# Decode attention with a gated MLP on one core: the first keys through two DMA queues, in halves of the partitions

## The chip, the core and the metric

The kernel runs on one core of a Trainium2 chip. The metric is the device time of one execution in microseconds. The kernel before takes 193.44 us (median of three runs, 193.33 to 193.98). All profile figures come from one profiled execution, and times inside it count from its first instruction. TensorE is PE (with PEld for its weight loads), VectorE is DVE, ScalarE is ACT, GpSimd is POOL and SyncE is SP. The suffix q (SPq, ACTq) means the sequencer that issues DMAs. SP and ACT each have a DMA queue of their own: q1 in the profile is SP's, q10 is ACT's.

## What is computed

One token (a row of 512) goes through a layer norm and then two branches: attention of 32 heads over the last 4096 positions of a key and value cache, and a small MLP. In the reference, cut to what matters:

```python
xn = _layernorm(x)
q = (xn @ wq).reshape(B, Sq, 32, 128)
W = 4096
k, v = k_cache[:, :, Sk - W:, :], v_cache[:, :, Sk - W:, :]
p = softmax(einsum("bhqd,bhkd->bhqk", q, k) * Dh ** -0.5)
s = einsum("bhqk,bhkd->bhqd", p, v).reshape(1, 1, 4096) @ wo
x1 = xn + shift(gelu(layernorm(xn) @ w1)) @ w2      # S = 1: the shifted rows are zero
g = silu(x1 + gelu(layernorm(x1) @ w3) @ w4)
out = x + s * g
```

Each of the 32 heads has 1 MiB of keys and 1 MiB of values, each read once. With the weights it is 79 MB in all, and little arithmetic on each byte.

## The kernel before, in words

The heads are worked in eight groups of four (G = 4, NG = 8). The keys of a group, K0 to K7 below, are one tile of 4 MiB, `kv` from `k_pool`: partition p = 4b + a holds positions 128b to 128b + 127 of head a, which is a row of 32 KB. The values V0 to V7 have the same form in `v_pool`. There are three key buffers (K_BUFS) and two value buffers (V_BUFS).

In the scores of a group, DVE takes the first 64 or 80 of the 128 positions of every partition: four times a product with the broadcast query (L321) and a sum over the 128 elements (L323), the function `k_vector`. PE takes the rest: it transposes pairs of positions (L339, `k_turn`), ACT copies them out (L342), and PE multiplies them with the query (L350, `k_scores`). Then follow the maximum (`sm_max`, L364 and L366), the exponential on ACT (`sm_exp`), the product with the values on PE (`v_wide`, L427) and the normalisation. A loop of NG + LAG = 10 steps writes the order out by hand for PE, DVE and ACT: in step s it works on the keys of group s and the values of group s - 2. In the last step the values of group 7 come in pieces (`cuts`, columns 0 to 64, 64 to 96 and 96 to 128), so that work starts on the first; the output weights of the last four heads come as rows (`load_rows`), and `y_head` multiplies with them.

Ahead of the loop stand the layer norms, the query (L208, from `wq`) and the MLP (L252 to L280). Their order on the engines is a scheduler's and not written out. The weights lie in a pool (`wts`) that is closed before V0 is loaded, since the value buffers take its place: so V0's load waits for all readers of the weights.

The loads have this order. ACT issues `x_bf`, `x_row` and `wq` (L79 to L84) and nothing more. SP issues w2, w3, w4 (1280 rows of it as 10 KB a partition, then 96 rows of 1 KB in one load of 96 partitions, L92), then K0 in two halves by columns (L534: positions 0 to 63 of each partition, then 64 to 127), K1, K2, V0, K3, V1, K4, V2 and so on. `keep_in_program_order` holds each queue to the order of the program. A load of keys from K3 on waits until the buffer of three groups before is read; a load of values waits for the buffer of two groups before. Loads share eight completion semaphores in turn, so a load can also wait until the eighth one before it has landed.

Of the kernel before, what the change touches and what calls it, by code (L numbers as in the profile page):

```python
# [8 lines left out]
P = 128  # L9
BF16 = mybir.dt.bfloat16  # L10
FP32 = mybir.dt.float32
ACT = mybir.ActivationFunctionType
ALU = mybir.AluOpType
# [5 lines left out]
G = 4  # L19
# [7 lines left out]
def kernel(  # L27
# [14 lines left out]
    nc = tc.nc  # L42
# [3 lines left out]
    _, H, Sk, Dh = A_k_cache.shape  # L46
# [3 lines left out]
    W0 = Sk - W  # L50
    assert W == 4096
    CP = G * W // P
    PB = P // G
# [3 lines left out]
    scale = float(Dh) ** -0.5  # L57


    k_pool = ctx.enter_context(tc.tile_pool(name="k", bufs=K_BUFS))  # L60
    kt_pool = ctx.enter_context(tc.tile_pool(name="kt", bufs=4))
    prod_pool = ctx.enter_context(tc.tile_pool(name="prod", bufs=1))
    const = ctx.enter_context(tc.tile_pool(name="const", bufs=1))
    small = ctx.enter_context(tc.tile_pool(name="small", bufs=1))
# [7 lines left out]
    wts_guard = tc.tile_pool(name="wts", bufs=1)  # L72
    wts = wts_guard.__enter__()

    def load(dst, src):
        return tc.keep_in_program_order(nc.sync.dma_start(out=dst, in_=src))  # L76

    x_bf = small.tile([P, KC], BF16, name="x_bf")
    nc.scalar.dma_start(out=x_bf[:], in_=A_x.rearrange("a b (p c) -> p (a b c)", p=P))  # L79
# [3 lines left out]
    wq_sb = wts.tile([P, KC, HD], BF16, name="wq_sb")  # L83
    nc.scalar.dma_start(out=wq_sb[:].rearrange("p c n -> p (c n)"),  # L84
                        in_=A_wq.rearrange("(a b c) n -> b a (c n)", a=4, c=KC))
    w2_sb = wts.tile([P, KC, D], BF16, name="w2_sb")
    load(w2_sb[:], B_w2.rearrange("(p c) n -> p c n", p=P))
    w3_sb = wts.tile([P, KC, F], BF16, name="w3_sb")
# [1 line left out]
    w4_sb = wts.tile([P, 11, D], BF16, name="w4_sb")  # L90
    load(w4_sb[:, 0:10, :], B_w4[0:10 * P, :].rearrange("(p c) n -> p c n", p=P))
    load(w4_sb[0:96, 10, :], B_w4[10 * P:F, :])  # L92


    def load_kv(pool, cache, g, cuts=(0, CP)):
        t = pool.tile([P, CP, Dh], BF16, tag="kv", name="kv")
        src = cache[0, G * g:G * g + G, W0:, :].rearrange("a (b c) d -> b a (c d)", b=PB)
        dst = t[:].rearrange("p c d -> p (c d)")
        for c0, c1 in zip(cuts, cuts[1:]):
            load(dst[:, c0 * Dh:c1 * Dh], src[:, :, c0 * Dh:c1 * Dh])  # L100
        return t
# [16 lines left out]
    nc.vector.tensor_copy(out=sel[:], in_=ident_bf[:, 0:P:32].unsqueeze(1).to_broadcast([P, PB, G]))  # L118
    ind = const.tile([P, 1], FP32, name="ind")
    nc.vector.tensor_reduce(out=ind[:], in_=ident_f[:, 0:P:32], axis=AX.X, op=ALU.max)  # L120
    neg_half = const.tile([P, 33], FP32, name="neg_half")
    nc.vector.memset(neg_half[:], -0.5)


# [27 lines left out]
    def rows_add(ps, col, w, last):  # L152
        k = col.shape[0]
        for j in range(KC):
            nc.tensor.matmul(ps[32 * j:32 * j + 1, :], lhsT=col, rhs=w[0:k, j * P:(j + 1) * P],
                             start=False, stop=last, skip_group_check=True)
# [60 lines left out]
    for b in range(2):  # L217
# [5 lines left out]
        for t in range(2):  # L223
            rows = slice(64 * t, 64 * t + 64)
            nc.scalar.copy(out=q_pair[rows, 4 * b:4 * b + 4, :, G * t:G * t + G].rearrange("p g l a -> p g a l"),
                           in_=qt_ps[rows].bitcast(BF16).rearrange("p g (a m l) -> p g a m l", a=G, l=2)[:, :, :, 0, :])
# [14 lines left out]
    xn_row = small.tile([P, P], FP32, name="xn_row")  # L241
# [26 lines left out]
    for i, (col, w) in enumerate(terms):  # L268
        r = 32 * (i % 4)
# [4 lines left out]
    h2_ps = ps_misc.tile([P, P], FP32, tag="misc", name="h2_ps")  # L274
    rows_open(h2_ps)
    rows_add(h2_ps, ind, hr, True)
    bv = small.tile([P, P], FP32, name="bv")
    nc.vector.tensor_tensor(out=bv[:], in0=xn_row[:], in1=h2_ps[:], op=ALU.add)
    g_row = small.tile([P, P], FP32, name="g_row")
    nc.scalar.activation(out=g_row[:], in_=bv[:], func=ACT.Silu)  # L280


    make_masks(16)
# [13 lines left out]
                            op=ALU.max)  # L297
    par_t = const.tile([1 + G, PB, G], FP32, name="par_t")
    nc.vector.tensor_scalar(out=par_t[:],
                            in0=ident_f[0:1 + G, 1:1 + G].unsqueeze(1).to_broadcast([1 + G, PB, G]),  # L300
# [26 lines left out]
    def batches(g):  # L327
        n, m = nd(g), CP - nd(g)
        k = -(-m // 8)
        edges = [n + 2 * (m // 2 * i // k) for i in range(k + 1)]  # L330
        return list(zip(edges, edges[1:]))
# [12 lines left out]
    def k_scores(g, b):  # L344
        kt = kts.pop(b)
        c0, c1 = batches(g)[b]
        for i in range((c1 - c0) // 2):
            c = c0 + 2 * i - nd(g)
            for l in range(2):
                nc.tensor.matmul(st[g]["sT"][:, c:c + 2, :].rearrange("p c a -> p (c a)"),  # L350
                                 lhsT=kt[:, i, l::2], rhs=q_pair[:, g, l, :], start=(l == 0), stop=(l == 1))
# [55 lines left out]
    def load_wo(i):  # L407
        h0, n = blocks[i]
        load(wo_blk[i], A_wo[h0 * P:(h0 + n) * P, :].rearrange("(p t) n -> p t n", p=P))
# [4 lines left out]
    def load_rows(h, n):  # L414
        load(wo_rows[:, h - h_part:h - h_part + n, :],
             A_wo[h * P:(h + n) * P, :].rearrange("(h p) n -> p h n", p=P))
# [108 lines left out]
    NG = H // G  # L525
# [5 lines left out]
    for s in range(NG + LAG):  # L531
        h = s - LAG
        last = h == NG - 1
        kn = load_kv(k_pool, A_k_cache, s, (0, 64, CP) if s == 0 else (0, CP)) if s < NG else None  # L534
        if s == LAG:
            wts_guard.__exit__(None, None, None)
            v_pool = ctx.enter_context(tc.tile_pool(name="v", bufs=V_BUFS))
            wo_blk[2] = v_pool.tile([P, 4, D], BF16, tag="wo_4", bufs=1, name="wo_4")
            wo_rows = v_pool.tile([P, H - h_part, D], BF16, tag="wo_rows", bufs=1, name="wo_rows")
        if last:  # L540
            v = load_kv(v_pool, A_v_cache, h, cuts)
            for r in (H - G, H - 2):
                load_rows(r, 2)
        elif h >= 0:
            v = load_kv(v_pool, A_v_cache, h)
        if h == 3:
            wo_24 = k_pool.tile([P, 32, D], BF16, tag="kv", name="wo_24")
            wo_blk[0], wo_blk[1] = wo_24[:, 0:16, :], wo_24[:, 16:24, :]
            load_wo(0)
        if h == 5:  # L550
            load_wo(1)
            load_wo(2)

        if s < NG:
            nb = len(batches(s))

            def keys(b0, b1):
                for b in range(b0, b1):
                    k_turn(s, kn, b)
                    if b > 0:  # L560
                        k_scores(s, b - 1)

            k_open(s)
            k_vector(s, kn, 0)
            keys(0, 2)
            if s == 7:
                v_turn(h - 1)
                v_add(h - 1)
                v_out(h - 1)
            elif s > 1:  # L570
                sm_den(s - 2)
                sm_rden(s - 2)
            elif s == 1:
                sm_max(0)
            k_vector(s, kn, 1)
            keys(2, 4)
            if s == 7:
                sm_den(h)
                sm_rden(h)
                keys(4, nb - 2)  # L580
                sm_turn(s - 1)
                keys(nb - 2, nb)
            else:
                if s > 0:
                    sm_turn(s - 1)
                keys(4, nb)
            k_scores(s, nb - 1)
            sm_own(s)
            if s == 7:
                k_vector(s, kn, 2)  # L590
                v_wide(h, v)
                sm_exp(s - 1)
                v_turn(h)
                y_open()
                k_vector(s, kn, 3)
                v_add(h)
                v_out(h)
                ox_spread(1)
                sm_max(s)
                continue  # L600
            if s > 0:
                sm_exp(s - 1)
            if h > 0:
                v_turn(h - 1)
            k_vector(s, kn, 2)
            if h >= 0:
                v_wide(h, v)
            if h > 0:
                v_add(h - 1)
                v_out(h - 1)  # L610
            if s == 6:
                ox_spread(0)
            k_vector(s, kn, 3)
            if s == 6:
                ox_pick(0)
            if s > 0:
                sm_max(s)
        elif s == NG:
            ox_pick(1)
            sm_turn(NG - 1)  # L620
            sm_exp(NG - 1)
            y_wide(1, False)
            sm_den(NG - 2)
            sm_rden(NG - 2)
            y_wide(0, False)
            warm(3)
            v_wide(h, v)
            sm_den(NG - 1)
            sm_rden(NG - 1)
            v_turn(h)  # L630
            v_add(h)
            v_out(h)
            ox_spread(2)
        else:
            v_open(h)
            warm(3)
            v_wide(h, v, cuts[1], last=False)
            ox_pick(2)
            y_wide(2, True)
            nc.scalar.copy(out=y_sum[:], in_=yr[0][:].rearrange("p j n -> p (j n)"))  # L640
            v_wide(h, v, cuts[2], cuts[1])
            v_turn(h)
            v_add(h)
            rows_add(y_ps, ind, y_sum, False)
            v_part(h, v, cuts[2], CP)
            v_out(h)
            for r in range(H - G, H):
                y_head(r)
# [36 lines left out]
```

## Time and profile before

| what | us |
|---|---|
| the profiled execution, whole | 193.34 |
| its span, first to last instruction | 191.2 |
| between the two (not in the span) | 2.14 |
| DVE busy | 150.9 |
| PE busy | 116.4 |
| ACT busy | 89.2 |
| DVE's first product of K0 (L321) starts | 26.09 |
| DVE's first product of K1 starts | 41.91 |
| DVE's last maximum of the scores (L366, group 7) starts | 170.29 |
| the product with the last piece of V7 (L461) starts | 186.38 |

The profile gives the busy time of each engine, the span in 40 slices with the share of the 16 DMA engines in use and the GB/s that they moved, the DMA queues with their packets, the chain of work that ended last, and the costliest groups of instructions. A line of a timeline holds the start, the length, the engine, the line of the code, the operation, what it writes and reads, how often, and in brackets how long its engine was idle before it and what ended the wait. A load is listed under the line of its helper `load`, L76. A packet in the queues is here one contiguous row in one partition, or the 4 bytes that count up a semaphore at the end of a load.

### The profile page before, as it was taken

The numbers are of one execution on the slowest core, as the hardware profiler recorded it, in microseconds if no ns is written. First come the engines' busy times: TensorE is split into PE (matmuls) and PEld (weight loads), VectorE is DVE, ScalarE is ACT, GpSimd is POOL, SyncE is SP. The second block draws the span as 40 slices with busy tenths as digits, with TensorE's granted clock in tenths as the row PEclk, the third lists the DMA queues.
The fourth block names the chain that finished last, engine by engine and source line by source line (L and its number), as shares of the span: only waits on it lengthen the run. The fifth ranks groups of instructions, "written<-read, shape, count | busy, mean of one in ns | idle before, by whom it ended". The sixth has DMA issues, their size and how long they took to land.

```text
span 191.2 us, 2839 instructions
## 1 busy us (share of the span) xinstructions
PE 116.4 (61%) x1159; PEld 74.2 (39%) x1159; DVE 150.9 (79%) x175; ACT 89.2 (47%) x191; POOL 2.3 (1%) x11
## 2 busy tenths in 40 slices
PE   1653754989825368256845772680888189739762
PEld 0430222767614334143334441540763077313322
DVE  1660159979999999999999999999999999980111
ACT  2001370888794076427464564542475148733120
POOL 2110000000000000000000000000000000000000
PEclk9999695555755557955695588557567858975998
DMA  6999999999999999999999999999999998999990
GB/s 211 447 430 404 431 418 439 439 439 437 432 434 439 432 429 432 432 439 432 422 432 432 418 422 418 452 439 435 439 432 434 435 432 372 471 425 405 420 371 32
DMA packets 4572, 79.02 MB, mean 413 GB/s; under 512 B 624, under 2 KB 1232, under 8 KB 1488
## 3 DMA queue, kind: packets, MB, share of 16 engines
q1 hardware_dynamic: 4264, 74.65, 91.6%
q10 hardware_dynamic: 296, 4.20, 5.1%
q8 instruction: 9, 0.15, 0.3%
q14 instruction: 3, 0.02, 0.0%
HBM read 78.84 MB, written 0.00 MB: 412 GB/s over the span
## 4 chain that ended last, share of the span: by engine, by line
DVE 46%; DMA 43%; PE 5%; ACT 3%; issue 1%; SPq 1%; ACTq 0%; DVEq 0%
DMA kv<-in_A_k_cache_dram 31%; DVE S L323 28%; DVE prod L321 15%; DMA kv<-in_A_v_cache_dram 10%; ACT kt L342 3%; DMA x_bf<-in_A_x_dram 2%; PE pt L339 2%; PE ov L427 1%; DVE m L366 1%; DVE S L364 1%; SPq L76 1%; PE sT L350 1%; DVE mx L374 1%; PE oT L461 1%; PE ot_ps L444 0%
## 5 line engine op out<-in xcount | busy, mean ns | idle before, releaser
L323 DVE TENSOR_REDUCE S<-prod 128x20 f32<-128x2560 bf16 (+1 forms) x32 | 86.0, 2686 | 1.1
L342 ACT COPY kt<-pt 128x1024 bf16<-128x1024 bf16 x52 | 51.2, 1013 | 40.4 <-PE pt L339 38.7
L339 PE MATMUL pt<-ident_f,kv 128*128 128x128 f32 x208 | 46.7, 376 | 10.8 <-DMA kv<-in_A_k_cache_dram 10.8
L321 DVE TENSOR_TENSOR prod<-kv,q_bc 128x2560 bf16<-128x2560 bf16 (+1 forms) x32 | 45.4, 1418 | 3.9 <-DMA kv<-in_A_k_cache_dram 3.7
L339 PEld LDWEIGHTS pt<-ident_f,kv 128*128 128x128 f32 x208 | 34.2, 196 | 14.4 <-DMA kv<-in_A_k_cache_dram 10.5
L350 PE MATMUL sT<-q_pair,kt 128*128 128x8 bf16 x416 | 19.4, 170 | 15.7 <-ACT kt L342 15.5
L350 PEld LDWEIGHTS <-kt 128*128 128x128 bf16 x416 | 16.4, 104 | 26.8 <-ACT kt L342 25.8
L427 PE MATMUL ov<-kv,pT 128*16 128x512 bf16 x248 | 22.0, 515 | 1.4 <-DMA kv<-in_A_v_cache_dram 1.4
L388 ACT ACTIVATE pT<-S,mb 128x128 bf16<-128x128 f32 x32 | 13.9, 573 | 0.3
L372 PE MATMUL mt_ps<-ident_f,m 128*1 128x128 f32 x8 | 2.9, 359 | 17.4 <-DVE rden L399 16.9
L433 ACT COPY ov_sb<-ov 128x512 f32<-128x512 f32 x8 | 4.7, 586 | 17.1 <-PE ov L427 17.1
L427 PEld LDWEIGHTS <-pT 128*16 128x16 bf16 x248 | 6.9, 109 | 13.2 <-issue 11.4
L359 ACT ACTIVATE own<-sT,par 128x48 f32<-128x48 f32 (+1 forms) x32 | 7.5, 356 | 3.7 <-PE sT L350 3.7
L444 PE MATMUL ot_ps<-ident_f,ov_sb 128*128 128x128 f32 x32 | 7.1, 359 | 2.9 <-ACT mb L384 1.9
L211 DVE CAST q_row<-qr_ps 128x512 bf16<-128x512 f32 x1 | 0.7, 692 | 9.9 <-PE qr_ps L208 9.9
L388 ACT ACTIVATION_READ_ACCUMULATOR pT<-S,mb 128x1 f32 x32 | 8.3, 258 | 0.0
L372 PEld LDWEIGHTS mt_ps<-ident_f,m 128*1 128x1 f32 x8 | 0.6, 80 | 17.9 <-DVE rden L399 17.2
L399 DVE RECIPROCAL rden<-den_ps 128x4 f32<-128x4 f32 x8 | 1.4, 175 | 7.0 <-PE den_ps L394 7.0
L381 PE MATMUL mb_ps<-md,par_t 5*128 5x4 f32 x16 | 3.9, 311 | 4.1 <-DVE md L376 4.1
L255 ACT ACTIVATE a_row<-a_ps 128x384 bf16<-128x384 f32 x1 | 0.5, 491 | 12.0 <-remote 12.0
L444 PEld LDWEIGHTS ot_ps<-ident_f,ov_sb 128*128 128x128 f32 x32 | 4.5, 178 | 3.9 <-ACT mb L384 2.3
L208 PE MATMUL qr_ps<-wq_sb,xq_bf 128*1 128x512 bf16 x32 | 3.1, 566 | 3.7 <-DMA wq_sb<-in_A_wq_dram 3.7
(122 smaller groups left out, 81.6 us busy)
## 6 DMA issues: line engine op xcount, KB each, us to landing
kv<-in_A_k_cache_dram SPq DMA_DIRECT2D x7, 4096.0 KB, 31.3
kv<-in_A_v_cache_dram SPq DMA_DIRECT2D x7, 4096.0 KB, 30.6
wq_sb<-in_A_wq_dram ACTq DMA_DIRECT2D x1, 4096.0 KB, 17.6
kv<-in_A_k_cache_dram SPq DMA_DIRECT2D x2, 2048.0 KB, 27.4
wo<-in_A_wo_dram SPq DMA_DIRECT2D x1, 2048.0 KB
kv<-in_A_v_cache_dram SPq DMA_DIRECT2D x1, 2048.0 KB
kv<-in_A_v_cache_dram SPq DMA_DIRECT2D x2, 1024.0 KB, 17.6
w_sb<-in_B_w_dram SPq DMA_DIRECT2D x1, 1376.0 KB, 9.1
```

Of the source, the lines that this page charges most:

```text
L321: nc.vector.tensor_tensor(out=prod[:, 0:m, :], in0=kn[:, rows, :], in1=q_bc[:, g:g + 1, :].to_broadcast([P, m, Dh]), op=ALU.mult)
L323: nc.vector.tensor_reduce(out=st[g]["S"][:, rows], in_=prod[:, 0:m, :], axis=AX.X, op=ALU.add)
L339: nc.tensor.transpose(pt[:, i, :], kn[:, c:c + 2, :].rearrange("p c d -> p (c d)").bitcast(FP32), ident_f[:])
L342: nc.scalar.copy(out=kts[b][:, 0:n, :], in_=pt[:, 0:n, :].bitcast(BF16))
L350: nc.tensor.matmul(st[g]["sT"][:, c:c + 2, :].rearrange("p c a -> p (c a)"), lhsT=kt[:, i, l::2], rhs=q_pair[:, g, l, :], start=(l == 0), ...
L359: nc.scalar.mul(s["own"][:, 0:m, a], s["sT"][:, 0:m, a], par[:, a:a + 1])
L372: nc.tensor.transpose(mt_ps[:], s["m1"][:], ident_f[:])
L381: nc.tensor.matmul(mb_ps[:], lhsT=par_t[:].rearrange("k b a -> k (b a)"), rhs=md[:], start=True, stop=True)
L388: nc.scalar.activation(out=s["pT"][:, :, a], in_=s["S"][:], func=ACT.Exp, scale=scale, bias=mb[:, a:a + 1], accum_out=s["sum"][:, a:a + 1])
L427: nc.tensor.matmul(ov[r:r + 4 * G], lhsT=s["pT"][:, c:c + 4, :].rearrange("p i a -> p (i a)"), rhs=v[:, c:c + 4, :], start=(i < 4), stop=( ...
L433: nc.scalar.copy(out=s["ov_sb"][:], in_=ov[:])
L444: nc.tensor.transpose(ot_ps[:, step * j:step * j + P], s["ov_sb"][:, j, :], ident_f[:])
```

## The change

1. A new pool `front` ahead of `k_pool` holds `neg_half`, now 32 values (128 bytes) wide. In the built program the key buffers begin at 16640, 49408 and 82176 bytes of each partition in place of 16512, 49280 and 82048: multiples of 256 in place of 128 bytes past one. `bv` is made 8 values wider so that the pools behind it, the value buffers among them, stay where they were (160000 and 192768, multiples of 256 before and after).
2. K0 and K1 are loaded before the loop in two halves each, by partitions: partitions 0 to 63 on SP's queue, 64 to 127 on ACT's. K2 is one load on ACT's queue. The two halves by columns of K0 are gone. From K3 on the loads are as before.
3. The last four heads' rows of `wo` are one load and not two of two heads.

The queues after it: SP has w2, w3, w4, the 96 rows of w4, K0 (lower half), K1 (lower half), V0, K3, V1 and so on. ACT has `x_bf`, `x_row`, `wq`, K0 (upper half), K1 (upper half), K2. In the built program K2's issue waits for `wq` to have landed, and ACT's first computing instruction is queued behind it. The scheduler moves some of the work ahead of the loop: on ACT the Gelu (L255) comes behind the copies of the query and has one more table load ahead of them; on PE two batches of K0's transposes now stand ahead of the last MLP products; on DVE the copy `a_bf` (L260) comes behind the first product and sum of K0, and `hr` (L273) behind the second. DVE's first product and PE's first transpose of K0 and of K1 now wait for both halves.

```diff
+    front = ctx.enter_context(tc.tile_pool(name="front", bufs=1))
     k_pool = ctx.enter_context(tc.tile_pool(name="k", bufs=K_BUFS))
...
-    def load(dst, src):
-        return tc.keep_in_program_order(nc.sync.dma_start(out=dst, in_=src))
+    def load(dst, src, engine=None):
+        return tc.keep_in_program_order((engine or nc.sync).dma_start(out=dst, in_=src))
...
+    kvs = {}
+
+    def keys_load(g, b0, b1, engine):
+        if g not in kvs:
+            kvs[g] = k_pool.tile([P, CP, Dh], BF16, tag="kv", name="kv")
+        load(kvs[g][G * b0:G * b1].rearrange("p c d -> p (c d)"),
+             A_k_cache[0, G * g:G * g + G, W0:, :].rearrange("a (b c) d -> b a (c d)", b=PB)[b0:b1], engine)
...
     load(w4_sb[0:96, 10, :], B_w4[10 * P:F, :])
+    keys_load(0, 0, PB // 2, nc.sync)
+    keys_load(0, PB // 2, PB, nc.scalar)
+    keys_load(1, 0, PB // 2, nc.sync)
+    keys_load(1, PB // 2, PB, nc.scalar)
+    keys_load(2, 0, PB, nc.scalar)
...
-    neg_half = const.tile([P, 33], FP32, name="neg_half")
+    neg_half = front.tile([P, 32], FP32, name="neg_half")
...
-    bv = small.tile([P, P], FP32, name="bv")
+    bv = small.tile([P, P + 8], FP32, name="bv")
...
-        kn = load_kv(k_pool, A_k_cache, s, (0, 64, CP) if s == 0 else (0, CP)) if s < NG else None
+        kn = kvs[s] if s in kvs else load_kv(k_pool, A_k_cache, s) if s < NG else None
...
-            for r in (H - G, H - 2):
-                load_rows(r, 2)
+            load_rows(H - G, G)
```

More of the change, by code (lines that the diff above doesn't have):

```diff
@@ L276 @@
     rows_add(h2_ps, ind, hr, True)
-    bv = small.tile([P, P], FP32, name="bv")
-    nc.vector.tensor_tensor(out=bv[:], in0=xn_row[:], in1=h2_ps[:], op=ALU.add)
+    bv = small.tile([P, P + 8], FP32, name="bv")
+    nc.vector.tensor_tensor(out=bv[:, 0:P], in0=xn_row[:], in1=h2_ps[:], op=ALU.add)
     g_row = small.tile([P, P], FP32, name="g_row")
-    nc.scalar.activation(out=g_row[:], in_=bv[:], func=ACT.Silu)
+    nc.scalar.activation(out=g_row[:], in_=bv[:, 0:P], func=ACT.Silu)
     make_masks(16)
```

## The prediction, made before the result was known

> **What bounds the kernel now.** I read the page's slices first, then the chain of work that ended last, then the timelines at both ends of the chain.
>
> ```profile
> DVE  1660159979999999999999999999999999980111
> ...
> DMA  6999999999999999999999999999999998999990
> ```
>
> From the second slice on the DMA engines are never free, and DVE is nearly full from the seventh to the 36th. Two things end together: 79.02 MB at some 432 GB/s, and DVE's scores. The chain of waits shows how they meet:
>
> ```profile
> 5.29 36.53 DMA kv<-in_A_k_cache_dram
> ...
> 130.25 23.26 DMA kv<-in_A_k_cache_dram
> ...
> 167.79 18.54 DMA kv<-in_A_v_cache_dram
> ```
>
> The first is K1 from issue to landing, then DVE without a gap for 88 us, then K7, then the last piece of V7. How close DVE is to the chain all the way, its timeline tells:
>
> ```profile
> 26.09 1.23 DVE L321 TENSOR_TENSOR prod<-kv,q_bc 128x2048 bf16<-128x2048 bf16 x1 [2.19 <-DMA kv<-in_A_k_cache_dram]
> ...
> 41.91 1.49 DVE L321 TENSOR_TENSOR prod<-kv,q_bc 128x2560 bf16<-128x2560 bf16 x1 [0.99 <-DMA kv<-in_A_k_cache_dram]
> ...
> 134.17 1.49 DVE L321 TENSOR_TENSOR prod<-kv,q_bc 128x2560 bf16<-128x2560 bf16 x1 [0.55 <-DMA kv<-in_A_k_cache_dram]
> ```
>
> After K0's first half has landed, DVE waits for keys only 0.99 us (K1) and 0.55 us (K6) in 144 us. At the end PE waits for V7:
>
> ```profile
> 181.50 1.04 PE L427 MATMUL ov<-kv,pT 128*16 128x512 bf16 x16 [1.02 <-DMA kv<-in_A_v_cache_dram]
> ...
> 183.93 0.61 PE L427 MATMUL ov<-kv,pT 128*16 128x512 bf16 x8 [0.41 <-DMA kv<-in_A_v_cache_dram]
> ```
>
> These 1.02 and 0.41 us are all the room between DVE's end of group 7 (170.58) and the last values. So a late DVE has 0.55 + 1.4 = 1.95 us of cover behind K1's start, and what exceeds it lengthens the kernel.
>
> **How two queues share the engines.** While `wq` (ACT, q10) and w4 (SP, q1) were both in flight, two stretches of the queue view (columns: packets, MB, share of 16 engines), the first 10.6 to 17.0 us, the second 9.4 to 10.6 us:
>
> ```profile
> q10 hardware_dynamic: 64, 2.10, 75.9%
> q1 hardware_dynamic: 64, 0.66, 24.1%
> ```
>
> ```profile
> q10 hardware_dynamic: 16, 0.52, 101.1%
> q1 hardware_dynamic: 16, 0.00, 0.8%
> ```
>
> The turns are one packet for one packet, whatever their size: 64 rows of 32 KB against 64 rows of 10 KB, and in the second stretch 16 rows of 32 KB against 16 packets without bytes to speak of, the semaphore counts that close w3's load. A queue with small packets gets few bytes.
>
> **What the Trainium skill says.** (1) "DMA: Bandwidth & Descriptors", section on queues, rings and completion order: an engine goes round robin between the rows it has work for, at packet granularity, a packet being typically 9 to 17 descriptors. The trace agrees with the turns, but here one row is a turn. (2) Same page, why a DMA increments its semaphore by 16: the slowest dimension decides over how many engines a load is split, 16 for 64 partitions. So each half gives each engine four rows. (3) "SBUF — State Buffer", Door 1: partitions 0 to 63 reach only 8 of the 16 ports, 196 GB/s at 1 MiB against 328 for all 128. No load of this trace covers half the partitions with long rows, so no row here shows it. (4) First page, how a descriptor splits: a start off a multiple of 256 bytes costs an extra partial transaction.
>
> **The change, part by part.** A 32 KB row at 432 GB/s over 16 engines takes 1.213 us (T).
>
> *Alignment.* Loads of keys at their old offset move 437 GB/s (K3, 60.5 to 68.0 us) and 428 (K4, 80.0 to 87.5); the values, aligned already, 429 (V0, 51.0 to 58.5) and 424 (V1, 70.5 to 78.0). Nothing to gain: 0, at most 0.3 us for small losses in the first loads.
>
> *One load of rows.* SP issues one DMA less (0.5 us) behind the last piece of V7, when SP has nothing else to do until the output at 188.68. The packets stay the same, and the heads' products (187.59) waited for DVE. 0; at worst 0.1 us.
>
> *The halves, in the queues.* `wq`'s last row goes at about 19.0 us. At that point SP's queue before still had two rows of w4, a semaphore, six rows of 1 KB per engine (96 partitions), a semaphore, and only then K0; ACT's queue was empty, so the small packets took 1 us together. Now ACT's queue holds eight key rows per engine (4 of K0, 4 of K1) and then K2. The small packets each give one turn to a key row of ACT's: nine turns of SP's without keys are enough for all eight. So the upper halves of K0 and K1 go first, and K0's lower half starts only behind them, then alternates with K2.
>
> With rows at the full rate: first upper row at 19.4, 8 x 1.213 = 9.7 plus 0.7 for the small packets: the lower half of K0 starts at 29.8. Its 4 rows with 3 of K2 between them are 7 x 1.213 = 8.5: 38.3. With 1.2 us for the slowest engine and the landing (`wq`: last row about 19.0, PE starts at 19.91) K0 is there at 39.5. K1's lower half: two rows of K2, then again seven: 49.2, landed 50.4.
>
> With half the ports: in the first stretch all engines write partitions 64 to 127 only, so a row takes 2T: 19.4 + 0.7, the lower half starts at 39.5; 4 x 2.43 + 3 x 1.21 = 13.3: 52.9, landed 54.1. K1: 52.9 + 2.4 + 13.3 = 68.6, landed 69.8. The unknown is the row's price, T to 2T; below T is excluded by the 432 GB/s that every saturated stage shows. I take 2T, [...]and keep T for the range.
>
> *On DVE.* Before, DVE started on K0 when half of it, by columns, had landed (26.09). Group 0 takes it to 40.92, 14.83 us with `hr` and `bv` in it. Now it starts at 54.1 and ends at 68.9; K1 is there at 69.8. So K1's start moves from 41.91 to 69.8, by 27.9 us. From there the chain is DVE's own. Less the cover of 1.95: +26.0 us.
>
> *The other issues.* K2's issue on ACT waits for `wq` (19.91), with ACT's table load and the query copies queued behind: 19.9 + 0.6 for the issue + 1.3 for the load = 21.8, the time at which the first copy started before (21.84): 0, and anything up to 30 us would be hidden by the wait for K0. The extra table load (1.3) and the Gelu stand in the same idle time. V0's issue waits for the MLP, which on DVE is behind two products of K0: 54.1 + 8.7 = 62.8, while the queues hold K1 and K2 until 68.6: 0. With full-rate rows it is 48.2 against 49.3, and the gap of about a microsecond falls where DMA is no longer last. The transfers lose 16 half-rate rows, 16 x 1.213 = 19.4 us; 186.4 + 19.4 is 206, well before DVE's chain ends, so this adds nothing more. The later loads waited 10 us or more behind others before (K6 issued at 112.03, its stretch of the queue began near 122), and DVE falls behind DMA by only 27.9 - 19.4 = 8.5.
>
> *Sum.* 191.2 + 26.0 = 217.2 span, + 2.14 = 219.3 on the profiled execution's 193.34. The median, 193.44, is 0.1 above it. I say 219.
>
> **The rivals.**
>
> (a) Turns as above, but a half load runs at the full rate: the engines, not the ports, set the rate. For it: the rate per engine (27 GB/s) is the same in every load of this trace, so ports were never seen to bind. Against it: the page's measurement. K0 at 39.5, DVE to 54.3, later than K1's 50.4; K1 starts 12.4 late; 12.4 - 1.95 = +10.5: 203.8. If each half used only its own eight engines, K2 would alternate with it instead, and K0 lands near 38: 202 to 203.
>
> (b) The two halves go in step, because a group of small packets takes one turn. Then K0 has landed when 11.25 MiB have moved: 2.3 + 27.3 + 1.0 = 30.6. DVE to 45.4, 3.5 late, less 1.95: +1.6, 195. Against it: the second queue stretch, where each semaphore packet had its turn.
>
> (c) Not slower: the last values set the end, and DVE's lag is hidden. This is (b) with more cover at the wait for V7 (181.50) than I count. It decides if the cover is at least 3.5 us, not 1.95. The end then stays the transfer's, with perhaps 0.3 us won at the first loads: 193.1. Against it: PE's idle times before V7 are only 1.4 us in sum, and (b) has to hold as well.
>
> (d) The change does nothing by its alignment or the joined rows: contained above, as both are costed at 0.
>
> **How the numbers follow.** Forecast, turns and half ports: 0.58 (own range 214 to 222). (a): 0.32 (201.5 to 206). Between the two, if rows sharing ports cost less than 2T: 0.05. (b): 0.03. (c): 0.02. The range takes in the forecast and (a), both ends of the row's price: 201.5 to 222. This kernel's measurement tells about 0.3% (0.6 us) from no change: faster 0.01, same 0.02, slower 0.97.
>
> **What would show it.** Right: DVE's first product of K0 near 54 with a wait of some 30 us for keys, that of K1 near 70, about 220 GB/s from 20 to 40 us with ACT's queue moving nearly all of it, DVE without waits for keys later, and V7 landed microseconds before PE needs it. For (a): 430 GB/s in that stretch and K0 near 39.5. For (b): both queues at equal bytes from 20 us on. Wrong altogether: DVE's first product before 30 us, or V7 still last.

## The result, and the profile after

| | before | after |
|---|---|---|
| median, us | 193.44 (193.33 to 193.98, five runs) | 224.92 (223.72 to 226.4, five runs) |
| the profiled execution, whole | 193.34 | 225.42 |
| its span | 191.2 | 223.3 |
| first product of K0 starts | 26.09 | 56.11 |
| first product of K1 starts | 41.91 | 74.37 |
| first product of K1 to the end of the span | 149.27 | 148.90 |

The ratio is 1.1625 (95% interval 1.157 to 1.1681): the kernel is 31.5 us slower. 219.0 was forecast, with a range up to 222, so the measured time lies above the range. The direction and both mechanisms were right; the loss is 6 us larger than the forecast. Of the runs of all kernels below, one took over 1.5% longer than the fastest of its kernel; it counts as slow and is left out.

The slices of the page after (DVE's and the DMA engines' busy tenths, then the GB/s moved), and below them the GB/s of the page before:

```profile
DVE  1720100000979699999999999999999999994011
...
DMA  7999999999999999999999999799999999957930
GB/s 238 449 434 341 250 197 194 282 282 282 282 279 276 445 387 459 429 423 449 405 458 434 414 423 411 335 379 423 423 420 423 436 443 420 431 252 282 420 147 3
```

```profile
GB/s 211 447 430 404 431 418 439 439 439 437 432 434 439 432 429 432 432 439 432 422 432 432 418 422 418 452 439 435 439 432 434 435 432 372 471 425 405 420 371 32
```

A slice is 5.6 us after and 4.8 us before. The DMA engines are as busy as before, but from the fifth slice to the 13th they move 194 to 282 GB/s where before they moved 418 to 439: a busy share says nothing of the rate. DVE stands idle from the sixth slice to the tenth. Two stretches after (columns: stretch, length, busy time of the engines with their instructions, granted clock, DMA share, GB/s), the first without and the second with rows of SP's halves:

```profile
24.00:39.00 15.00, 1.94 (x12) 1.09 (x11) 0.07 (x1) 4.93 (x10) 0.00 (x0) 0.59 1.02 216
39.00:54.00 15.00, 0.00 (x0) 0.00 (x0) 0.00 (x0) 0.00 (x0) 0.00 (x0) 0.50 1.04 280
```

The queues after from 24 to 39 us (packets, MB, share of 16 engines):

```profile
q10 hardware_dynamic: 112, 3.15, 97.9%
q1 hardware_dynamic: 112, 0.10, 3.8%
```

ACT's 112 packets are 96 rows of 32 KB and 16 semaphore counts, SP's are 96 rows of 1 KB and 16 counts: one for one. In the raw packets ACT's key rows last 2.36 to 2.50 us here, most of them 2.44 to 2.46, where a row took 1.213 us before. SP's first row of K0 starts at 39.24; 39.5 was forecast.

DVE's timeline after shows what came of it:

```profile
56.11 1.22 DVE L336 TENSOR_TENSOR prod<-kv,q_bc 128x2048 bf16<-128x2048 bf16 x1 [32.04 <-DMA kv<-in_A_k_cache_dram]
...
66.14 0.29 DVE L293 TENSOR_TENSOR bv<-xn_row,h_ps 128x128 f32<-128x128 f32 x1 [1.17 <-PE h_ps L170]
...
74.37 1.49 DVE L336 TENSOR_TENSOR prod<-kv,q_bc 128x2560 bf16<-128x2560 bf16 x1 [2.17 <-DMA kv<-in_A_k_cache_dram]
```

Two waits for keys, 32.04 and 2.17 us, and none for K2 to K7. The chain of waits has both, but can't name what released them:

```profile
24.07 31.91 another core or an unknown queue
...
72.20 2.09 another core or an unknown queue
```

There is no other core: the pieces have the times of DVE's two waits, and the timeline's brackets say which data they were for. V7 is not in the chain any more. PE's timeline after, at its last values:

```profile
214.30 1.04 PE L442 MATMUL ov<-kv,pT 128*16 128x512 bf16 x16
...
216.15 0.60 PE L442 MATMUL ov<-kv,pT 128*16 128x512 bf16 x8
```

The brackets with 1.02 and 0.41 us of waiting for V7 are gone.

### The profile page after: what moved, and what is told of

The parts are those of the page before. It is cut to its first block, busy times and chain, and to the rows that moved or that the text cites. A ratio compares the mean times of both kernels' runs of the same rounds, so it can differ in the third digit from the quotient of the medians.

```text
span 223.3 us, 2841 instructions
## 1 busy us (share of the span) xinstructions
PE 120.2 (54%) x1159; PEld 74.2 (33%) x1159; DVE 151.0 (68%) x175; ACT 90.3 (40%) x192; POOL 2.3 (1%) x11
## 4 chain that ended last, share of the span: by engine, by line
DVE 59%; another core or an unknown queue 15%; PE 13%; DMA 8%; ACT 2%; issue 1%; ACTq 0%; POOL 0%; DVEq 0%; POOLq 0%
DVE S L338 35%; DVE prod L336 17%; DMA wq_sb<-in_A_wq_dram 8%; PE ov L442 3%; PE pt L354 2%; PE qr_ps L223 2%; PE yr_ps L533 1%; DVE S L379 1%; DVE m L381 1%; PE wm L522 1%; ACT kt L357 1%; PE ot_ps L459 1%; PE hr_ps L285 1%; DVE mx L389 1%
## 5 line engine op out<-in xcount | busy, mean ns | idle before, releaser
L354 PE MATMUL pt<-ident_f,kv 128*128 128x128 f32 x208 | 44.9, 363 | 31.0 <-DMA kv<-in_A_k_cache_dram 27.6
L354 PEld LDWEIGHTS pt<-ident_f,kv 128*128 128x128 f32 x208 | 32.9, 189 | 35.1 <-issue 35.1
L365 PE MATMUL sT<-q_pair,kt 128*128 128x8 bf16 x416 | 19.4, 170 | 18.0 <-ACT kt L357 17.8
L442 PE MATMUL ov<-kv,pT 128*16 128x512 bf16 x248 | 24.9, 570 | 0.0
L442 PEld LDWEIGHTS <-pT 128*16 128x16 bf16 x248 | 7.1, 117 | 14.1 <-issue 13.3
L396 PEld LDWEIGHTS mb_ps<-md,par_t 5*128 5x128 f32 x16 | 3.6, 279 | 7.9 <-PE sT L365 4.6
## 6 DMA issues: line engine op xcount, KB each, us to landing
kv<-in_A_v_cache_dram SPq DMA_DIRECT2D x7, 4096.0 KB, 20.1
kv<-in_A_k_cache_dram SPq DMA_DIRECT2D x2, 2048.0 KB, 69.8
```

The costliest lines, as they stand in the source:

```text
L354: nc.tensor.transpose(pt[:, i, :], kn[:, c:c + 2, :].rearrange("p c d -> p (c d)").bitcast(FP32), ident_f[:])
L396: nc.tensor.matmul(mb_ps[:], lhsT=par_t[:].rearrange("k b a -> k (b a)"), rhs=md[:], start=True, stop=True)
L442: nc.tensor.matmul(ov[r:r + 4 * G], lhsT=s["pT"][:, c:c + 4, :].rearrange("p i a -> p (i a)"), rhs=v[:, c:c + 4, :], start=(i < 4), stop=( ...
```

## Theory and rivals

The theory after the result: (1) turns, packet for packet, let ACT's upper halves go ahead of SP's K0; (2) a half by lower or upper partitions runs at half the rate, because its rows share ports of the destination; (3) the forecast mis-sized what comes behind these. Rivals: one of the two causes alone; the side that is read, not the ports written; the size or the partition count of a load; a third cause, such as the moved offsets or the changed order of work ahead of the loop.

## Experiments: the parts alone

**Alignment and the joined rows only** (on the kernel before).

```diff
+    front = ctx.enter_context(tc.tile_pool(name="front", bufs=1))
...
+    neg_half = front.tile([P, 32], FP32, name="neg_half")
...
+    bv = small.tile([P, P + 8], FP32, name="bv")
...
+            load_rows(H - G, G)
```

> The kernel before with the first and third part of the change alone: key buffers at multiples of 256 bytes, the last four heads' rows as one load; all keys on SP's queue, K0 in halves by columns, as before. Theory (the loss is all in the half loads on two queues; alignment and joined rows are worth nothing): within 0.3 us of before, 193.4 us, and rows of keys at 1.21 us, K0 at 26. Rival (the alignment or the joined load carries a part of the 31 us, or wins some tenths against it): off by 0.6 us or more on either side.

193.4 us, ratio 1.0004 (0.9989 to 1.0019). Parts 1 and 3 of the change cost and bring nothing; all of the loss is in the loads of K0 to K2.

**Halves by columns**, on the same two queues in the same order:

```diff
-    keys_load(0, 0, PB // 2, nc.sync)
-    keys_load(0, PB // 2, PB, nc.scalar)
+    cols_load(0, 0, 64, nc.sync)
+    cols_load(0, 64, CP, nc.scalar)
```

and K1 likewise; `cols_load` takes positions 0 to 63, or 64 to 127, of all partitions.

> The changed kernel with K0 and K1 halved by columns (positions 0 to 63 on SP, 64 to 127 on ACT) in place of partitions: the same bytes on the same two queues in the same order, but every load covers all 128 partitions, as 16 KB rows. Theory (half the partitions reach half the ports, so a half load runs at half the rate; on top the turns hold SP's keys back): the rate from 20 us on is 430 GB/s and no longer 200; ACT's eight rows of K0 pass SP's small packets, K0's first half lands at 36, DVE's group 1 starts at 51 to 52, 9.5 to 10.3 late, 202 to 203 us. Rival 1 (two queues of large loads slow the engines as such): about 210 GB/s from 20 to 40 us as in the changed kernel and over 215 us. Rival 2 (no turns, only ports): K0 lands near 31 and 195 us.

204.19 us, ratio 1.0541 (1.0517 to 1.0565). From its second slice (5.1 us each) up to the start of K0 at 36.97 it moves 402 to 487 GB/s:

```profile
GB/s 206 487 406 402 451 418 459 456 382 414 456 448 421 409 427 427 450 395 466 414 417 414 434 414 236 414 434 479 417 427 414 419 403 458 459 84 398 406 79 3
```

So 20.7 of the 31.5 us depend on how the tile is halved, and 10.8 remain with all rows at the full rate.

**The same halves, all on SP's queue**:

```diff
-    keys_load(0, PB // 2, PB, nc.scalar)
+    keys_load(0, PB // 2, PB, nc.sync)
```

and the other two of ACT's likewise.

> The changed kernel with all halves by partitions (and K2) on SP's queue, one behind the other: half loads without a second queue. Theory (ports): each half runs at 216 GB/s, K0 lands at 40.7 and K1 at 60.2; the transfers lose 16 x 1.213 = 19.4 us and set the end: 212.7 us. Rival 1 (two queues slow each other, a half load on its own does not lose): 430 GB/s, K0 at 31, 194 to 195 us.

213.49 us, ratio 1.103 (1.1013 to 1.1047). The half rate needs no second queue:

```profile
24.00:48.00 24.00, 8.27 (x78) 5.72 (x76) 6.63 (x6) 7.44 (x12) 0.00 (x0) 0.64 1.03 218
```

Here the end is the transfers' own: the last piece of V7 is in at 205.27, before at 185.93, 19.3 us later. The forecast had 19.4 for 16 half-rate rows.

**Whole loads, K0 on SP, K1 and K2 on ACT**:

```diff
+    keys_load(0, 0, PB, nc.sync)
+    keys_load(1, 0, PB, nc.scalar)
     keys_load(2, 0, PB, nc.scalar)
```

> The changed kernel with whole loads on the two queues: K0 on SP, K1 and K2 on ACT, no halves. Theory (the turns alone, at full rate): while SP's queue goes through two rows of w4, its 1 KB rows and semaphore counts, one for one with ACT's rows of 32 KB, K1 is loaded ahead of K0; K0 starts near 30, alternates with K2 and lands at 49; DVE's group 1 starts at 64 to 65, 22 to 23 late; behind it 0.4 us of cover as the changed kernel showed or 1.95 as I counted: 214 to 216 us, with DMA at 430 GB/s throughout. Rival 2 (turns do not matter, queues share bytes evenly): K0 and K1 alternate from 20 us, K0 at 40.6, 205 to 207 us. Rival 1 (two queues as such halve the rate): over 230 us.

219.54 us (218.49 to 220.6), ratio 1.1347 (1.131 to 1.1384): 26 us lost with every row at the full rate, since all of K1 and more goes ahead of K0, which is in use at 51.47. Expected were 49 and 214 to 216. The first row of K0 starts at 31.26, where nine turns put it (19.4 + 9 x 1.213 + 0.7 = 31.0); the last engine's semaphore count came a turn behind the others, at 50.97 against 49.4 to 49.9 (by the times of the raw packets, another queue's packet of 16 KB took a turn on that engine, from 30.10 to 31.07; step 3 below has another such case).

```profile
GB/s 215 433 475 438 405 394 485 388 479 12 0 194 429 430 432 436 412 439 424 424 448 427 418 430 403 206 460 412 457 388 448 426 403 467 412 182 364 410 102 3
```

The 12 and 0 are a gap in the transfers themselves: both queues are empty and V0 waits for the MLP, which DVE does behind K0.

## Experiments: is it the ports?

**Halves by even and odd partitions**, on the same two queues in the same order. Each load still has 64 partitions and four rows of 32 KB for each engine. It also reads other rows of the source; what that is worth, the run after it tests:

```diff
-        load(kvs[g][G * b0:G * b1].rearrange("p c d -> p (c d)"),
-             A_k_cache[0, G * g:G * g + G, W0:, :].rearrange("a (b c) d -> b a (c d)", b=PB)[b0:b1], engine)
+        load(kvs[g][a0:P:step].rearrange("p c d -> p (c d)"),
+             A_k_cache[0, G * g + a0:G * g + G:step, W0:, :].rearrange("a (b c) d -> b a (c d)", b=PB), engine)
```

> The changed kernel with K0 and K1 each halved by even and odd partitions instead of lower and upper: the same two queues, in the same order, 64 partitions, four rows of 32 KB for each engine in every load. Half the ports: even and odd partitions both reach all ports, so rows take 1.21 us, only the turns are left, K0 at about 37 and 203 to 205 us, as for the halves by columns. If 64 partitions, or the size of the loads, halve the rate: 224 to 229 us, as the changed kernel.

208.2 us, ratio 1.0767 (1.0748 to 1.0786). ACT's rows alone, beside SP's small packets, and the first product of K0:

```profile
20.00:30.00 10.00, 5.62 (x45) 2.06 (x37) 0.69 (x1) 6.80 (x12) 0.00 (x0) 0.68 1.00 430
```

```profile
41.38 1.22 DVE L336 TENSOR_TENSOR prod<-kv,q_bc 128x2048 bf16<-128x2048 bf16 x1 [17.49 <-DMA kv<-in_A_k_cache_dram]
```

430 GB/s, every row 1.213 us: neither 64 partitions nor the size of the load halves the rate, but which 64. The Trainium skill ("SBUF — State Buffer", Door 1) gives a map in which partitions 32 apart share a port and the upper 64 have the other eight; even partitions reach all 16. The measurement agrees: 430 against 216 GB/s. The ports themselves are the page's account; the runs show that the rate depends on which partitions are written. The time missed the expected 203 to 205, because K0 came at 41.38 and not at 37, the figure taken over from the halves by columns, whose rows are half as long and whose turns are therefore shorter. In the raw packets K0's last row ends at 39.65, but its last semaphore count goes through only at 40.86, behind one more row of ACT's (see step 3 below).

**Other source rows for the same halves**: each half reads every second block of 128 positions.

```diff
+            src = src.rearrange("a (b t c) d -> t b a (c d)", t=2, b=PB // 2)[b0 // (PB // 2)]
```

> The changed kernel, same queues and same halves of the partitions, but each half reads every second block of source rows instead of a half of the source; the positions of the keys of groups 0 and 1 thereby stand in another order than those of their values, so that the attention of these eight heads is changed and its time is not. Ports of the destination: unchanged, 224 to 226 us, rows of 2.4 us in the stretch of 24 to 39 us. If the side that is read is what halves the rate: rows of 1.2 us, 204 to 206 us.

227.58 us (226.7 to 228.98, three runs), and from 24 to 38 us the rows last 2.38 to 2.51 us again:

```profile
24.00:38.00 14.00, 2.02 (x13) 1.09 (x11) 0.29 (x1) 4.93 (x10) 0.00 (x0) 0.63 1.10 232
```

Which rows are read, then, makes no difference to the rate. That the kernel is another 2.7 us slower than the changed one was not expected. In its profile K0 is used at 60.07: 15 of the 16 semaphore counts of its lower half have gone through by 56.5, the last comes at 59.34. Why that one engine lags stays open.

**Quarters of 32 partitions, all on SP**:

```diff
+    for g in range(2):
+        for b in range(0, PB, PB // 4):
+            keys_load(g, b, b + PB // 4, nc.sync)
```

> K0 and K1 in four loads of 32 partitions each, and K2, all on SP's queue in order. Ports: [...]rows still take 2.4 us and the time is that of the halves on one queue, 212 to 215 us. If the rate goes down with the number of partitions or of rows for each engine: rows of 4.9 us, K0 and K1 taking some 39 us longer than in halves, above 245 us.

228.76 us, ratio 1.1836 (1.1792 to 1.188), between the two expectations, and for another reason than either:

```profile
21.00:27.00 6.00, 6.00 (x53) 2.72 (x45) 0.86 (x2) 4.11 (x10) 0.00 (x0) 0.64 0.53 221
```

Half of the DMA engines are busy (0.53), with rows of 1.213 us; the others stand idle from about 20.5 to 27.6 us although all four quarters of K0 were issued by 7.1 us, and start only after K2, a whole load, has been issued (25.7). So such a load uses eight engines, and, since the other eight stay free, the same eight each time. The skill ("DMA: Bandwidth & Descriptors", on how many engines a load uses, in the section on why a DMA increments its semaphore by 16) says that the slowest dimension decides; here it is eight blocks. So this run can't tell ports from counts.

## Experiments: turns, and the order in the queues

**Even and odd partitions, all on SP**: the three ACT issues of the even-odd kernel go to SP.

> The changed kernel with K0 and K1 halved by even and odd partitions and all five loads on SP's queue in order: neither a second queue nor half the ports. Both causes are then gone, and only the halves by columns are missing that let DVE start early: K0 in use near 32 us, 197 to 198 us, as the kernel before with K0 in one piece. If a third cause is left in the changed kernel: above 199 us.

198.18 us, ratio 1.024 (1.0197 to 1.0282); K0 in use at 32.17. Its stretch from 21 us on, and its first product of K0:

```profile
21.00:40.00 19.00, 13.62 (x125) 8.60 (x118) 9.54 (x9) 11.07 (x17) 0.00 (x0) 0.68 1.01 435
```

```profile
32.17 1.23 DVE L336 TENSOR_TENSOR prod<-kv,q_bc 128x2048 bf16<-128x2048 bf16 x1 [3.87 <-DMA kv<-in_A_k_cache_dram]
```

With this the causes stand in a square (us; in brackets, above the kernel before, 193.4):

| | lower and upper halves | even and odd halves |
|---|---|---|
| two queues | 224.9 (+31.5) | 208.2 (+14.8) |
| SP's queue only | 213.5 (+20.1) | 198.2 (+4.8) |

The ports are worth 15.3 us on one queue and 16.7 on two; the second queue 10.0 at the full rate and 11.4 at half. 4.8 us remain without either: K0 is no longer used from its first half by columns on.

**The kernel before with K0 in one piece** tests that, and the cover that the forecast counted:

```diff
-        kn = load_kv(k_pool, A_k_cache, s, (0, 64, CP) if s == 0 else (0, CP)) if s < NG else None
+        kn = load_kv(k_pool, A_k_cache, s, (0, CP)) if s < NG else None
```

> The kernel before with K0 as one load instead of two halves by columns: DVE starts on K0 when all of it has landed, near 31 instead of 26, and K1 starts some 4 us later than 41.9. With the cover that the forecast counted, 1.95 us: 195.3 to 195.8 us. With the 0.15 to 0.4 us that the shifted kernels have shown: 197.0 to 197.6 us.

197.53 us, ratio 1.0227 (1.0207 to 1.0247). K1 starts at 46.49 instead of 41.91, 4.58 us late, and the median is 4.1 us longer, as with the small cover, not the counted one (in the profiled run, the fastest of five, the span is 3.6 us longer):

```profile
46.49 1.49 DVE L321 TENSOR_TENSOR prod<-kv,q_bc 128x2560 bf16<-128x2560 bf16 x1
```

The even-odd kernel on SP's queue took 198.2 (197.3 to 198.9), this one 197.5 (197.0 to 198.2): the spreads overlap, so nothing clear of noise is left for a third cause.

**w4's 96 small rows ahead of w3** in SP's queue, first in the even-odd kernel:

```diff
+    load(w4_sb[0:96, 10, :], B_w4[10 * P:F, :])
     w3_sb = wts.tile([P, KC, F], BF16, name="w3_sb")
     load(w3_sb[:], B_w3.rearrange("(p c) n -> p c n", p=P))
...
-    load(w4_sb[0:96, 10, :], B_w4[10 * P:F, :])
```

> The changed kernel with the halves by even and odd partitions, and with w4's 96 rows of 1 KB loaded before w3. If the small packets' turns are what lets ACT's queue ahead: ACT's key rows get ahead by 4 or 5 instead of 8, K0's rows on SP's queue start near 25 us instead of 29.9, K0 is in use near 36 instead of 41.4, and the kernel takes 201.5 to 204 us. If they don't matter: 208 us, as with the small rows in their place.

202.59 us, ratio 1.0472 (1.0441 to 1.0502): 5.6 us are won by moving 96 KB of the 79 MB. K0's rows start at 25.07 instead of 29.89, K0 is in use at 35.47. Turns are what the small packets give away.

The same edit in the changed kernel:

> The changed kernel with w4's 96 rows of 1 KB loaded before w3 instead of after w4's other rows; so between w4 and the lower half of K0 SP's queue holds no small packets but semaphore counts. Turns and half ports: ACT's queue gets ahead by two or three rows at most, after that upper and lower halves alternate in step, each pair at the price of two full rows. Both halves of K0 have then landed near 44 us instead of 56, K1 near 61, and the kernel takes 212 to 216 us; the transfers still lose some 19 us for the first stretch, where only ACT's few rows ran alone. If the turns given away to small packets don't matter: unchanged, 225 us, K0 at 56.

218.45 us, ratio 1.1286 (1.1239 to 1.1333): 6.5 us won, and not the 9 to 13 expected. K0's lower half starts at 29.69 instead of 39.24, as it should; but then lower and upper rows alternate at 2.25 us for each, not for the pair, and K0 is used at 49.80. The expectation had assumed that with both halves in flight all ports are used. In the raw packets 12 engines are on one queue's rows and four on the other's, and change together: engines that have come into step stay in step, so at any time most of them write the same half. That alone doesn't give the 2.25 us: an estimate from 1.213 us for a row is 1.8 us for 12 engines on eight ports, and 1.2 us for four on the other eight, but the rows of all 16 took about 2.25 us. The rest stays open.

**K2 behind the lower halves on SP's queue**:

```diff
-    keys_load(2, 0, PB, nc.scalar)
+    keys_load(2, 0, PB, nc.sync)
```

> The changed kernel with K2 issued on SP's queue behind the lower half of K1, so that no row of K2 stands between the lower halves. If K2's turns beside half-rate rows cost what the forecast missed: lower half of K0 alone from 39.5 us, four rows at 2.43 us, so K0 at about 51, K1 at about 61; DVE ends group 0 at about 67, and the kernel takes 217 to 220 us. If K2's turns are not the reason for the late K0 and K1: 224 to 226 us.

218.22 us, ratio 1.1294 (1.1254 to 1.1335): 6.7 us won. K0 is used at 51.20 and K1 at 67.32, both as worked out:

```profile
51.20 1.23 DVE L336 TENSOR_TENSOR prod<-kv,q_bc 128x2048 bf16<-128x2048 bf16 x1 [26.84 <-DMA kv<-in_A_k_cache_dram]
```

The last row of K0 ends at 50.24, and DVE starts 0.96 us later; in the changed kernel, with K2's rows between, 2.23 us later.

## Why the prediction was right in kind and 6 us short

The span is 223.3 where the sum gave 217.2. Two terms of the sum were mis-sized: when K0 and K1 can be used (step 3, 4.6 us) and the cover at the end (step 5, 1.6 us). Step by step:

1. *Alignment, joined rows: 0.* Right (1.0004).
2. *The order in the queues: nine turns for eight rows, half the ports, lower half from 39.5.* Right: 39.24, rows of 2.44 to 2.46 us, most of them, against 2.43. To take 2T, where the trace had no such load, was the decisive choice, and in part luck: the two rates that the prediction quotes, 196 and 328 GB/s, differ by a factor of 1.7. Full-rate rows, rival (a), were the even-odd kernel; it takes 208.2 where the rival gave 203.8, short by the steps 3 to 5 as well.
3. *"4 x 2.43 + 3 x 1.21 = 13.3", and "1.2 us for the slowest engine and the landing".* This step failed, for K0 and K1. The prices of the rows were both wrong, and it is luck that they nearly cancel: beside each other K2's rows last 1.5 to 2.1 us and not 1.21, the lower rows 1.7 to 2.3 and not 2.43, and a pair takes 3.8 instead of 3.64 us. And the 1.2 us was read from `wq`, at whose end only rows of 0.385 us of the other queue stood in the way. A semaphore count is a packet too, and waits its turn: the last row of K0 ends at 53.88 (forecast 52.9), the counts go through at 54.98 to 55.47, behind one more row of K2, and DVE starts at 56.11 (forecast 54.1): 2.0 us. For K1 it goes on: from K0's last row to the start of the last engine's first row of K1 2.9 instead of 2.4 us; the rows themselves 13.6 instead of 13.3 us, which brings 15 engines to 70.46; and the 16th is 2.7 us behind them, with its count at 73.12. By the times of the raw packets, another queue took a turn on that engine, which the forecast had at nothing: a packet of 16 KB of the queue that the profile calls instruction, from 62.62 to 63.99, between a row of K1 and one of K2. The queues after from 62.5 to 64.1 us:

```profile
q10 hardware_dynamic: 8, 0.26, 55.0%
q1 hardware_dynamic: 6, 0.20, 43.9%
q8 instruction: 1, 0.02, 5.4%
```

K1 starts at 74.37 instead of 69.8: 4.6 us, namely 1.0 for K0's last row, 0.5, 0.3 and 2.7 for the three parts above, and 0.1 from the last count to the start. K0's own late count isn't added, since it is part of the 2.9 us.

4. *Group 0 on DVE, 14.83 us.* 16.1, with 1.17 us of waiting for the MLP, now behind K0. No loss: 56.11 + 16.1 = 72.2, and K1's 2.17 us of waiting came after it.
5. *"0.55 + 1.4 = 1.95 us of cover".* 0.37. From K1's start to the end the kernel before takes 149.27 us, after 148.90. This step failed too. In the other shifted kernels whose end is DVE's chain it is 148.3 to 149.8, and the kernel with K0 in one piece lost 4.1 of its 4.6 us by the medians. The 0.55 us at K6 was won (K1 to K7 112.16 before, 111.53 after). Behind the last maximum 0.90 of the 1.4 us was won (19.99 instead of 20.89), but group 7, from its first product to that maximum, takes 17.38 us instead of 16.22, 1.16 more. In sum 0.63 + 0.90 - 1.16 = 0.37. PE's product with V5 (the first column is its start, the second its length), before and after:

```profile
164.60 1.90 PE L427 MATMUL ov<-kv,pT 128*16 128x512 bf16 x32
```

```profile
197.19 3.59 PE L442 MATMUL ov<-kv,pT 128*16 128x512 bf16 x32
```

DVE waits for it:

```profile
202.24 0.22 DVE L465 TENSOR_REDUCE oT<-ot_ps 128x4 f32<-128x64 f32 x1 [0.97 <-PE ot_ps L459]
```

The product's length goes with the clock that PE was granted, the third number from the end in these lines of the stretch of the product, before and after:

```profile
164.60:166.50 1.90, 1.90 (x36) 0.77 (x33) 1.86 (x2) 1.00 (x4) 0.00 (x0) 1.00 1.19 504
```

```profile
197.20:200.80 3.60, 3.60 (x36) 1.06 (x33) 3.53 (x3) 0.99 (x4) 0.00 (x0) 0.50 0.40 173
```

Full clock for 1.90 us, half for 3.59. This isn't due to the loads of the change. In the kernel with alignment and joined rows only the clock in that stretch was 0.59, the product took 3.16 us and group 7 17.71, and the whole was no longer than before: its tail behind the maximum was 19.76 instead of 20.89 us. There PE didn't wait for V7's first two pieces either, and the product with the last piece started at 186.45, as before (186.38). In the kernel before with K0 in one piece, which has nothing of the change but that K0's halves by columns are gone, the clock was 0.50 and the product took 3.59 us. So the time in front of V7 isn't free cover: PE's varying clock uses it, and while V7 comes last that doesn't show. The 1.95 us were read from an execution that had the full clock just there. Why it was granted there and not in the others was not tested.

6. *V0's issue, the other issues, the extra table load: 0.* Nothing in the trace speaks against it: V0 is issued at 66.17, behind the MLP, while K1's rows were on the way until 73.

Steps 3 and 5, 4.6 + 1.6 us, make up the 6.1 us that the forecast fell short, within rounding.

## What to carry to other kernels

Between two DMA queues an engine shares turns, not bytes: small rows and semaphore counts ahead of an urgent load each let a whole long row of the other queue pass, and the load's own count waits a turn at its end; so keep an urgent load on a queue whose rival is empty, or put small packets elsewhere. Halve a tile by columns or by even and odd partitions, not by lower and upper ones; two complementary halves in flight didn't make up for it. A wait of an engine that vanishes under a shift is cover only if what lies before it doesn't vary, so look at the granted clock in that stretch too: the time from the shifted point to the end, over two or three kernels, tells what the cover is worth.

## What was not expected of the hardware

- Engines in step: with lower and upper halves in flight at once, rows still took 2.25 us (210 to 240 GB/s).
- Rows of a whole tile beside lower-half rows lasted 1.5 to 2.1 us instead of 1.213, and the lower-half rows 1.7 to 2.3 instead of 2.45.
- Loads of 32 partitions in eight blocks ran on the same eight engines each time (0.53 busy, 221 GB/s), with the others idle beside a full queue.
- A semaphore count took about a turn of the other queue's rows: 2.23 us from last row to use with K2 between, 0.96 without.
- One packet of 16 KB of the instruction queue (1.37 us) left one engine 2.7 us behind the other 15, and the load's last count with it.
